# A linear-attention and dense-block kernel: w_in loaded 512 columns at a time, unit one's own term as products, and another written order

## The chip, the cores and the metric

The kernel runs on one core of a Trainium2 chip. A core has TensorE (PE, with its weight loads shown apart as PEld), VectorE (DVE), ScalarE (ACT), GpSimd (POOL) and SyncE (SP), each with an instruction queue of its own, and 16 DMA engines. The metric is the device time of one execution in microseconds (us), as the median of several runs.

## What is computed

Two blocks follow each other. The first is a linear attention with decay, over 4 batches, 8 heads, 768 steps and a head size of 48; the second is a dense block on its 3072 x 384 output:

```python
for t in range(S):
    kt, vt, rt = (k[:, :, t], v[:, :, t], r[:, :, t])
    cur = np.einsum('bhd,bhe->bhde', u[None] * kt, vt)
    y[:, :, t] = np.einsum('bhd,bhde->bhe', rt, state + cur)
    state = w[None, :, :, None] * state + np.einsum('bhd,bhe->bhde', kt, vt)
...
h = x @ w_in            # 384 -> 2048
g = h - np.tanh(h)
return (g @ w_out).astype(np.float32)
```

r, k, v, w and u are float32; w_in and w_out come as float64 (6.3 MB each) and are turned into float32 on the chip. The term with u, `cur`, is called the own term here: it adds to each step's output what the step's own k and v give.

## The kernel before, in words

**Units.** A unit is 64 steps of two batches with all heads; there are 24. Its chain: r, k and v are loaded (`fetch`, L644, two transfers each, one for each batch; for units zero and one one of them is ACT's, otherwise both are SP's); TensorE transposes r and k (`turn`, L656); DVE scales r with the powers of w into rT (L660) and ACT or DVE makes kT (L692, L665); TensorE multiplies rT with the state (`from_state`) and rT with kT (`levels`); DVE copies the products under the causal mask into `at` (L830); TensorE multiplies `at` with v (`outputs`) and k with v (`to_state`), all of these through `put`, L606; ACT copies the outputs into `xt` and `rest` (L765), and DVE or ACT updates the state (L792, L795). From unit twelve on r and k come already spread over DVE's transposes.

**The own term** has two forms. Units with a number under `OWN` (L35) use products: ACT multiplies kT by w times u (`own_k`, L709, four instructions), TensorE makes 16 more products (`own_levels`), and DVE copies their diagonal into `at` (L821). The others multiply r, k and u on DVE (L696, L824), sum over the head (L700), and ACT writes the diagonal (`diagonal`, L704, eight instructions).

**Tiles.** A tile is a block of two units' outputs (256 rows) by 256 columns of w_in. TensorE makes h in two halves of three products each (L217); ACT makes an arctan, two tanh, a square and a relu (L229 to L235); DVE makes g (L242 to L246); TensorE multiplies g with w_out (L254, or L307 in a form with seven products for eight, whose sums POOL prepares). The first six blocks are gone through in three passes over 4, 4 and 8 of the sixteen groups of 128 columns, the other six one by one.

**Weights.** w_in and w_out come in 16 pieces (`Weights`): for each n, n % 4 of 0 and 1 are 256 columns of w_in each, 2 and 3 are 256 rows of w_out. A piece of w_in comes in four transfers, alternately issued by SP (48 partitions, 288 KB) and POOL (16 partitions, 96 KB), in rows of 256 x 8 bytes, into one of four staging buffers `st`. `convert` turns it into float32: DVE twice (L185, L186), ACT twice (L187, L188), DVE three times (L189 to L191).

**What sets the order.** `lay_out` makes a list of tasks, each an engine's step with the tasks it comes after. The string `ORDER` (L45) then names them one by one, two characters each, and `Plan.written` emits them in that order; so each engine's queue is that order, restricted to the engine. An instruction waits for what it reads and for what it overwrites. Numbers beyond the tasks stand for the fillings: products of the identity with itself (`fills`, L534, 512 or 256 columns) that nobody reads, and one for reading the flag that chooses a general path. Transfers of SP and ACT take turns at eight counters; each waits until the transfer eight before it, of either, has landed.

## Time and profile before

| | us |
|---|---|
| runs shown: median, lowest, highest (3) | 582.31, 581.24, 583.12 |
| the profiled execution | 582.57 |
| its span, first to last instruction | 580.8 |
| busy: PE, DVE, ACT, POOL | 562.5, 429.9, 404.3, 199.9 |
| HBM read, written | 31.66 MB, 4.72 MB |
| mean granted TensorE clock | 0.998 |

The profiled execution gives the page and the trace; times in them count from the span's start. A row of a timeline has the start, the time taken, engine, line, operation and tiles, and in brackets the idle time ahead of it with what ended it. `x4` counts instructions; each product of float32 operands shows as two, and some records can be missing. In the chain of work, "issue" is time in which an engine waited for nothing that the profile shows. A busy engine may be one whose instructions are long; TensorE's ends are modelled.

### The profile page before, as it was taken

The numbers are of one execution on the slowest core, as the hardware profiler recorded it, in microseconds if no ns is written. First come the engines' busy times: TensorE is split into PE (matmuls) and PEld (weight loads), VectorE is DVE, ScalarE is ACT, GpSimd is POOL, SyncE is SP. The second block draws the span as 40 slices with busy tenths as digits, with TensorE's granted clock in tenths as the row PEclk, the third lists the DMA queues.
The fourth block names the chain that finished last, engine by engine and source line by source line (L and its number), as shares of the span: only waits on it lengthen the run. The fifth ranks groups of instructions, "written<-read, shape, count | busy, mean of one in ns | idle before, by whom it ended". The sixth has DMA issues, their size and how long they took to land.

```text
span 580.8 us, 14137 instructions
## 1 busy us (share of the span) xinstructions
PE 562.5 (97%) x5487; PEld 480.4 (83%) x5487; DVE 429.9 (74%) x720; ACT 404.3 (70%) x926; POOL 199.9 (34%) x366
## 2 busy tenths in 40 slices
PE   7699999999999999999999999999999999999995
PEld 4467777777776789999888889989999988999994
DVE  4899878999998787967699796567676766454534
ACT  2699999999977566545884787577577568765550
POOL 5201111300000233546256184273455253463430
PEclk9999999999999999999999999999999999999999
DMA  8987857594620000132344451441233000010001
GB/s 137 171 199 145 140 117 118 120 173 109 142 64 5 1 1 1 28 56 44 54 67 85 61 105 23 68 89 17 45 63 61 2 21 16 5 30 2 19 11 32
DMA packets 138549, 38.48 MB, mean 66 GB/s; under 512 B 130761, under 2 KB 132905, under 8 KB 138473
## 3 DMA queue, kind: packets, MB, share of 16 engines
q1 hardware_dynamic: 130140, 29.71, 28.7%
q0 software_dynamic: 4992, 6.99, 5.3%
q10 hardware_dynamic: 3340, 0.79, 0.9%
q8 instruction: 45, 0.74, 0.5%
q14 instruction: 32, 0.25, 0.2%
HBM read 31.66 MB, written 4.72 MB: 63 GB/s over the span
## 4 chain that ended last, share of the span: by engine, by line
PE 87%; DMA 4%; ACT 3%; DVE 2%; issue 1%; SPq 1%; POOL 0%; ACTq 0%; DVEq 0%; POOLq 0%
PE h L217 41%; PE p L307 26%; PE o L254 10%; PE yk_ps L606 6%; DMA rt<-in_r_dram 2%; PE x_ps L656 1%; DMA vt<-in_v_dram 1%; DMA xt<-rest 1%; ACT at L704 1%; PE x_ps L606 1%; SPq L644 1%; ACT xt L765 0%; PE p L254 0%; PE x_ps L534 0%; POOL xt L786 0%
## 5 line engine op out<-in xcount | busy, mean ns | idle before, releaser
L217 PE MATMUL h<-xt,w_in_sb 128*128 128x256 f32 x1152 | 267.3, 381 | 0.2 <-DMA xt<-rest 0.2
L217 PEld LDWEIGHTS h<-xt,w_in_sb 128*128 128x128 f32 x1152 | 214.9, 190 | 32.5 <-DVE g L242 1.5
L290 POOL TENSOR_TENSOR sg<-g 128x256 f32<-128x256 f32 x69 | 55.1, 800 | 197.7 <-DVE g L246 130.1
L242 DVE TENSOR_TENSOR g<-h,th 128x512 f32<-128x512 f32 x96 | 65.8, 686 | 67.9 <-ACT tg L233 25.2
L229 ACT ACTIVATE s<-h 128x512 f32<-128x512 f32 x96 | 57.1, 594 | 54.3 <-PE h L217 47.2
L307 PE MATMUL p<-mixed,sg 128*128 128x192 f32 x426 | 92.3, 327 | 0.0
L244 DVE TENSOR_TENSOR tg<-s,tg 128x512 f32<-128x512 f32 x96 | 69.3, 724 | 29.2 <-ACT s L224 19.4
L233 ACT ACTIVATE tg<-h 128x512 f32<-128x512 f32 x96 | 56.9, 594 | 41.9 <-PE h L217 29.9
L246 DVE COPY_PREDICATED g<-small,tg 128x512 f32<-128x512 int32 x96 | 72.0, 761 | 12.0 <-ACT small L235 9.0
L231 ACT ACTIVATE th<-h 128x512 f32<-128x512 f32 x96 | 56.7, 593 | 32.7 <-PE h L217 32.6
L307 PEld LDWEIGHTS p<-mixed,sg 128*128 128x128 f32 x426 | 73.3, 190 | 1.3 <-issue 0.3
L307 PE MATMUL p<-w_out_sb,g 128*128 128x192 f32 x284 | 70.4, 330 | 0.3 <-DVE o L335 0.3
L235 ACT ACTIVATE small<-s,smallb 128x512 f32<-128x512 f32 x96 | 68.5, 721 | 1.2
L254 PE MATMUL o<-w_out_sb,g 128*128 128x384 f32 x192 | 67.3, 489 | 0.0
L786 POOL DMA_DIRECT2D xt<-rest x66 | 32.5, 496 | 91.7 <-ACT rest L765 91.1
L224 ACT ACTIVATE s<-s 128x512 f32<-128x512 f32 x96 | 60.7, 633 | 1.4
L307 PEld LDWEIGHTS p<-w_out_sb,g 128*128 128x128 f32 x284 | 50.6, 190 | 3.1 <-DVE o L335 0.6
L254 PEld LDWEIGHTS o<-w_out_sb,g 128*128 128x128 f32 x192 | 35.8, 190 | 19.4 <-DVE parts L267 0.2
L704 ACT ACTIVATE at<-same,du 128x64 f32<-128x64 f32 x184 | 48.2, 342 | 0.5 <-DVE du L700 0.4
L292 POOL TENSOR_TENSOR sg<-sg,g 128x128 f32<-128x128 f32 x69 | 39.1, 569 | 3.1
L294 POOL TENSOR_TENSOR sg<-sg,g 128x128 f32<-128x128 f32 x69 | 37.2, 542 | 3.4
L307 PE MATMUL p<-mixed,g 128*128 128x192 f32 x142 | 34.7, 326 | 0.0
(127 smaller groups left out, 654.1 us busy)
## 6 DMA issues: line engine op xcount, KB each, us to landing
st<-in_moe_w_out_dram SPq DMA_DIRECT2D x8, 768.0 KB, 5.5
st<-in_moe_w_in_dram SPq DMA_DIRECT2D x16, 288.0 KB, 5.9
rt<-in_r_dram SPq DMA_DIRECT2D x46, 96.0 KB, 3.6
vt<-in_v_dram SPq DMA_DIRECT2D x46, 96.0 KB, 3.7
kt<-in_k_dram SPq DMA_DIRECT2D x44, 96.0 KB, 3.2
out_dram<-o POOLq DMA_DIRECT2D x44, 96.0 KB, 2.2
st<-in_moe_w_in_dram POOLq DMA_DIRECT2D x16, 96.0 KB, 5.9
parts<-in_k_dram SPq DMA_DIRECT2D x48, 32.0 KB, 2.1
```

Of the source, the lines that this page charges most:

```text
L217: self.nc.tensor.matmul(t.h2[:, z], self.w_in_sb[:, t.f // 2, kk, z * 128 : (z + 1) * 128], self.xts[t.j][:, kk].rearrange("p b t -> p (b ...
L224: A.activation(t.s, t.s, AF.Square, scale=G3)
L229: A.activation(out, t.h, AF.Arctan, scale=G2)
L231: A.activation(out, t.h, AF.Tanh)
L233: A.activation(out, t.h, AF.Tanh, scale=G1)
L235: A.activation(out, t.s, AF.Relu, bias=self.smallb, scale=-1.0)
L242: V.tensor_tensor(t.g, t.h, t.th, ALU.subtract)
L244: V.tensor_tensor(t.tg, t.s, t.tg, ALU.mult)
L246: V.copy_predicated(t.g, t.small.bitcast(I32), t.tg)
L254: self.nc.tensor.matmul(self.outs[i], t.g2[:, z, i * C : (i + 1) * C], self.w_out_sb[:, t.f + z, :], start=t.first and z == 0, stop=t.last ...
L290: add(t.s4[:, :2], g[:, 0::3], g[:, 1:2].to_broadcast([128, 2, C]), ALU.add)
L307: self.nc.tensor.matmul(ps[bank][:, half * n : (half + 1) * n], a, b, start=t.first and half == 0, stop=t.last, skip_group_check=True)
```

## The change

Three edits. First, `OWN` is 2, so unit one's own term takes the form with products too. Second, where w_in is float64, the two pieces of 256 columns next to each other share one set of four transfers with rows of 512 x 8 bytes, into one staging buffer `si` of twice the size; w_out has two buffers `so`. The four transfers of the first pair are all SP's; in later pairs the smaller two stay POOL's. A pair's transfers come after the conversion of both pieces of the pair before. A piece is then converted from its half of the buffer, in the same steps. Third, `ORDER` is another string throughout; it has 11 fillings (four of 512 columns, six of 256, and the flag's reading) where there were 16 (nine, six and the flag's reading).

```diff
-OWN = 1
+OWN = 2
...
-    "00010J2f2g2h2i2j2k2l2m2n0HbWbX02030K040605bWbWbW2o2q3534363231332r2t0I2s07370A0FbWbX080B0C2u2x2y38392v092w3U0D3C"
+    "00012P2Q2R0K2W2T2S2UbEbF02030I042V2X06bF2Y2o2n2p050A0H0C2a2r2q2s072c082b0B2d2e0J2h092f2u2i2Z2w2g0D3A0EbF2y3D2j3C"
...
-        return self.w_in_sb[:, of], parts
+        return parts
+
+    def wide(self, n):
+
+        return n % 4 < 2 and self.sources[0].dtype == I64
 
     def load(self, n, i, queue):
 
-        dst, parts = self.piece(n)
-        if self.sources[n % 4 > 1].dtype == I64:
+        if self.wide(n):
             if n not in self.staged:
-                self.staged[n] = self.stage.tile([128, self.COLS], I64, name="st", tag="st", bufs=4)
-            dst = self.staged[n].rearrange("p (k f) -> p k f", k=dst.shape[1])
+                self.staged[n] = self.staged[n + 1] = self.stage.tile([128, 2 * self.COLS], I64, name="si", tag="si", bufs=1)
+            dst = self.staged[n].rearrange("p (k f) -> p k f", k=self.d.NK)
+            parts = self.spread(self.sources[0][:, n // 4 * 512 : (n // 4 + 1) * 512])
+        else:
+            dst, parts = self.piece(n)
+            if self.sources[n % 4 > 1].dtype == I64:
+                if n not in self.staged:
+                    self.staged[n] = self.stage.tile([128, self.COLS], I64, name="so", tag="so", bufs=2)
...
+        if self.wide(n):
+            st = st[:, :, n % 2 * 256 : (n % 2 + 1) * 256]
...
-            queues, data = (("SP",), (3.0,)) if n % 4 > 1 else (("SP", "POOL") * 2, (1.2, .95) * 2)
-            of = [add(e, .55, lambda n=n, i=i, e=e: weights.load(n, i, e_of[e]), [converted[n - 4] if n >= 4 else None],
-                      data=x, gated=True) for i, (e, x) in enumerate(zip(queues, data))]
+            wide, freed = weights.wide(n), [converted[n - 4]] if n >= 4 else []
+            queues, data = (("SP",), (3.0,)) if n % 4 > 1 else (("SP", "SP" if n < 2 else "POOL") * 2, (1.3, .98) * 2 if wide else (1.2, .95) * 2)
+            if not wide or n % 4 == 0:
+                of = [add(e, .55, lambda n=n, i=i, e=e: weights.load(n, i, e_of[e]), freed + ([converted[n - 3]] if wide and freed else []),
+                          data=x, gated=True) for i, (e, x) in enumerate(zip(queues, data))]
```

`spread` is the old lines that cut w_in's columns into four parts, as a function. All lines behind them have numbers higher by 13 to 15 in the changed kernel (L606 is L621, L217 is L230, L534 is L547).

SP's queue at its start, before. `rt_106`, `rt_107`, `rt_108` are r of units zero, one and two, `first_k_122` and `_123` k of zero and one, `vt_116` and `_117` v of the same, `kt` k of later units, `ub` u, `st` w_in's staging buffer.

```order
L547 DMA rows<-in_w_dram 4x2x48
L171 DMA st<-in_moe_w_in_dram 48x3x256
L644 DMA rt_106<-in_r_dram 64x8x48
L644 DMA first_k_122<-in_k_dram 64x8x48
L644 DMA vt_116<-in_v_dram 64x8x48
L171 DMA st<-in_moe_w_in_dram 48x3x256
L644 DMA first_k_123<-in_k_dram 64x8x48
L644 DMA rt_107<-in_r_dram 64x8x48
L644 DMA vt_117<-in_v_dram 64x8x48
L568 DMA ub<-in_u_dram 128x384
L644 DMA kt<-in_k_dram 64x8x48 x2
L171 DMA st<-in_moe_w_in_dram 48x3x256
```

The same queue after, behind the first two of the list (`rows` and unit zero's r):

```order
L183 DMA si<-in_moe_w_in_dram 16x3x512
L659 DMA first_k_122<-in_k_dram 64x8x48
L183 DMA si<-in_moe_w_in_dram 16x3x512
L659 DMA vt_116<-in_v_dram 64x8x48
L659 DMA rt_107<-in_r_dram 64x8x48
L183 DMA si<-in_moe_w_in_dram 48x3x512
L659 DMA first_k_123<-in_k_dram 64x8x48
L183 DMA si<-in_moe_w_in_dram 48x3x512
L659 DMA rt_108<-in_r_dram 64x8x48
L659 DMA kt<-in_k_dram 64x8x48 x2
L581 DMA ub<-in_u_dram 128x384
L659 DMA vt_117<-in_v_dram 64x8x48
```

The first pair of w_in pieces now goes out whole ahead of unit one's v; in the row behind these the second half of unit two's r follows.

TensorE from unit zero's outputs to the first dense product, before. `x_ps_150` is the bank of unit one, `x_ps_146` that of units zero and two, `at_133` the masked products of unit one, `h<-ident` a filling.

```order
L606 MATMUL yk_ps<-vt_116,kw_112 64x48 x16
L534 MATMUL h<-ident 128x512
L534 MATMUL h<-ident 128x256
L606 MATMUL x_ps_150<-rT,kT 64x64 x16
L534 MATMUL h<-ident 128x256
L656 MATMUL x_ps_146<-ident,kw_112 128x128 x4
L656 MATMUL x_ps_146<-ident,rt_108 128x128 x4
L606 MATMUL yk_ps<-at_133,vt_117 64x64 x12
L606 MATMUL yk_ps<-at_133,extra_131 64x64 x12
L606 MATMUL yk_ps<-vt_117,kw_113 64x48 x16
L217 MATMUL h<-xt,w_in_sb 128x256 x3
```

And after:

```order
L621 MATMUL yk_ps<-vt_116,kw_112 64x48 x16
L621 MATMUL x_ps_150<-rT,kT 64x64 x16
L547 MATMUL h<-ident 128x512 x2
L671 MATMUL x_ps_146<-ident,kw_112 128x128 x4
L621 MATMUL x_ps_150<-rT,kU 64x64 x16
L671 MATMUL x_ps_146<-ident,rt_108 128x128 x4
L621 MATMUL yk_ps<-at_133,vt_117 64x64 x12
L621 MATMUL yk_ps<-at_133,extra_131 64x64 x12
L621 MATMUL yk_ps<-vt_117,kw_113 64x48 x16
L230 MATMUL h<-xt,w_in_sb 128x256 x3
```

Unit one's own products have come in, and the fillings stand behind its levels; unit two's r is still turned ahead of unit one's outputs.

DVE between unit one's scaling of r and its own copy, after (before, the two conversion steps of one piece stood here, and unit one's rk steps). `si` is w_in's buffer with both pieces.

```order
L675 TENSOR_TENSOR rT<-x_ps_150,power 128x512
L198 TENSOR_SCALAR power<-si 128x768
L199 TENSOR_SCALAR w_in_sb<-si 128x768
L198 TENSOR_SCALAR power<-si 128x768
L199 TENSOR_SCALAR w_in_sb<-si 128x768
L822 TENSOR_TENSOR kw_112<-kt,w_down 128x8x48
L845 COPY_PREDICATED at_133<-before,x_ps_150 128x512
L202 SCALAR_TENSOR_TENSOR w_in_sb<-w_in_sb,si 128x768
L836 COPY_PREDICATED at_133<-same,x_ps_150 128x512
```

The first steps of both pieces now stand ahead of the masked copies of unit one.

More of the change, by code (lines that the diff above doesn't have):

```diff
@@ L177, in convert @@
         V, A = self.nc.vector, self.nc.scalar
[L178 to L183 removed]
+        dst, st = self.piece(n)[0], self.staged.pop(n).rearrange("p (k f) -> p k f", k=self.piece(n)[0].shape[1])
+        if self.wide(n):
+            st = st[:, :, n % 2 * 256 : (n % 2 + 1) * 256]
+        words = st.bitcast(U32).rearrange("p k (f t) -> p k f t", t=2)
+        lo, hi = words[..., 0], words[..., 1]
+        lo_f = st.bitcast(F32).rearrange("p k (f t) -> p k f t", t=2)[..., 0]
+        power = self.stage.tile([128, self.COLS], U32, name="power", tag="power", bufs=2).rearrange("p (k f) -> p k f", k=dst.shape[1])
         bits = dst.bitcast(U32)
```

97 lines of the change are left out of this document (46 added, 51 removed).

## The prediction

> **What bounds the kernel now.** I read the page first: engine totals, the line of clock shares, the chain that ended last.
>
> ```profile
> span 580.8 us, 14137 instructions
> PE 562.5 (97%) x5487; PEld 480.4 (83%) x5487; DVE 429.9 (74%) x720; ACT 404.3 (70%) x926; POOL 199.9 (34%) x366
> PEclk9999999999999999999999999999999999999999
> PE 87%; DMA 4%; ACT 3%; DVE 2%; issue 1%; SPq 1%; POOL 0%; ACTq 0%; DVEq 0%; POOLq 0%
> ```
>
> TensorE is busy for 97% of the span, and 87% of the chain is its own. So a change can save only where TensorE does no useful work. A table by stretches shows where that is, and the same table for line 534 alone shows the products with the identity that only fill a wait.
>
> ```profile
> 25.40:55.70 30.30, 27.26 (x540) 20.52 (x536) 27.80 (x50) 29.44 (x86) 3.43 (x7) 1.00 0.91 182
> 55.70:100.00 44.30, 42.89 (x846) 33.17 (x846) 36.39 (x65) 42.29 (x126) 8.63 (x18) 1.00 0.66 118
> 100.00:150.00 50.00, 50.00 (x315) 36.80 (x314) 46.97 (x74) 47.16 (x98) 6.94 (x14) 1.00 0.65 139
> 150.00:580.80 430.80, 423.47 (x3492) 378.07 (x3490) 302.66 (x503) 275.60 (x594) 170.12 (x287) 1.00 0.22 39
> sum 50.00, PE 13.51 PEld 5.63; mean PE 1.35 PEld 0.56
> ```
>
> Columns: the stretch and its length, busy time of PE, PEld, DVE, ACT and POOL (instructions in brackets), granted clock, DMA share, GB/s; the last row is line 534 in the first 50 us. From 55.7 us TensorE lacks 1.4 us up to 100, nothing up to 150, and 7.3 us after that, most of it the end of the program. The loss sits ahead of 55.7: 13.5 us of filling, and idle time. From 25.4 to 55.7 DVE (27.8 of 30.3 us) and ACT (29.4) are as full as TensorE, and TensorE's 27.3 hold fillings. The chain in order of time says what holds the start:
>
> ```profile
> 4.19 6.26 DMA vt<-in_v_dram
> 15.20 7.33 DMA rt<-in_r_dram
> 22.66 0.63 PE x_ps L656 x4
> 23.29 0.90 PE yk_ps L606 x48
> 24.22 0.50 ACT xt L765
> 24.76 0.68 PE yk_ps L606 x32
> 25.44 1.49 PE h L217 x6
> 27.56 2.21 issue
> 29.77 0.69 PE x_ps L606 x32
> ```
>
> Unit two's r lands at 22.53; its transposes stand on TensorE ahead of unit one's outputs (23.29), from which ACT makes xt (24.22), and the first dense product starts at 25.44. At 27.56 TensorE stands for 2.21 us for nothing that the profile shows.
>
> **The change, part by part.** *Fewer fillings.* They fall from nine of 512 columns and six of 256 to four and six. TensorE's rows:
>
> ```profile
> 16.99 1.56 PE L534 MATMUL h<-ident 128*128 128x512 f32 x4
> 19.02 0.69 PE L606 MATMUL x_ps<-rT,kT 48*64 48x64 f32 x32 [0.47 <-DVE kT L665]
> 33.89 2.74 PE L534 MATMUL x_ps<-ident 128*128 128x512 f32 x6
> 42.45 0.59 PE L534 MATMUL x_ps<-ident 128*128 128x256 f32 x2
> 43.56 0.69 PE L606 MATMUL yk_ps<-rT,state 48*64 48x64 f32 x32 [0.52 <-DVE state L792]
> ```
>
> Three of 512 take 2.74 us, so five fewer are 5 x 0.91 = 4.6 us. But the filling of 16.99 ends at 18.55 and the next product still waits 0.47 us for DVE; the one of 42.45 likewise, 0.52. They cover waits that exist without them, so I cost their removal at nothing by itself: it is a gain only where the waits shorten. 4.6 us is the upper bound if they all do.
>
> *Unit one's own term.* What goes and what comes is shown by rows of units zero and one:
>
> ```profile
> 12.63 0.97 PE L606 MATMUL x_ps<-rT,kU 48*64 48x64 f32 x32 [1.01 <-ACT kU L709]
> 13.66 0.75 DVE L821 COPY_PREDICATED at<-same,x_ps 128x512 f32<-128x512 int32 x1 [1.19 <-PE x_ps L606]
> 15.23 0.55 DVE L696 TENSOR_TENSOR rk<-rt,first_k 128x384 f32<-128x384 f32 x1
> 17.23 0.55 DVE L824 TENSOR_TENSOR rk<-rk,ub 128x384 f32<-128x384 f32 x1
> 17.82 0.55 DVE L700 TENSOR_REDUCE du<-rk 128x8 f32<-128x384 f32 x1
> 18.41 2.02 ACT L704 ACTIVATE at<-same,du 128x64 f32<-128x64 f32 x8 [0.38 <-DVE du L700]
> 11.92 0.40 ACT L709 ACTIVATE kU<-kT,w_u 128x128 f32<-128x128 f32 x1 [1.58 <-POOL w_u L564]
> 12.23 0.97 ACT L709 ACTIVATE kU<-kT,w_u 128x128 f32<-128x128 f32 x3
> ```
>
> DVE loses 3 x 0.55 and gains 0.75: -0.9. ACT loses 2.02 and gains 0.40 + 0.97: -0.7. TensorE gains 16 products, 0.69 to 0.97 us, in a stretch where it fills: nothing on the path.
>
> *w_in.* Four transfers fetch what eight did; rows of 4 KB replace 2 KB; the first four are all SP's, where POOL issued half. Bytes stay. DVE's conversions are the same four large steps a piece. SP's queue changes: the w_in transfers now stand ahead of unit one's k, of u and of unit one's v, and unit two's r is split, its second half behind them all. At most eight transfers of SP and ACT are under way; in the program that second half waits until ACT's half of unit one's v has landed.
>
> ```profile
> 12.00 0.60 ACTq L644 DMA_DIRECT2D vt<-in_v_dram  x1
> 17.52 0.39 POOL L739 COPY extra<-vt 128x96 f32<-128x96 f32 x1 [4.39 <-DMA vt<-in_v_dram]
> DMA to landing us min/median/max: 2.7/4.4/7.4
> DMA to landing us min/median/max: 3.4/5.9/7.7
> ```
>
> The last two rows are r's and w_in's transfers. ACT's half of v is issued at 12.00, behind the same ACT steps in both, and has landed by 17.52. So unit two's r goes out at about 17.5 and, at the median 4.4, lands at 21.9 where it landed at 22.53: -0.6 us. Bounds: 2.7 gives 20.2, but then unit one's own copy on DVE decides. I put the last w_in issue at 10 us (SP's issues are 0.6 us each, with the landings they wait for); at the median 5.9 it lands at 16. Between that and the own copy DVE has four conversion steps (0.55), unit two's kw (0.55), the masked copy (0.75), a step of 0.95 and the copy itself: about 4.9 us with overlaps, so 21 us at best, -1.5. The maximum 7.4 gives 24.9, +2.4. I take -0.6, the median's.
>
> [...]
>
> *The order behind the first product.* I compare the same place in both: unit five's masked copy on DVE and the outputs behind it (TensorE, 55.68). Both orders have done seven half tiles of h and two of o by then.
>
> ```profile
> 24.00 0.69 DVE L660 TENSOR_TENSOR rT<-x_ps,power 128x512 f32<-128x512 f32 x1 [1.36 <-ACT kT L692]
> 54.04 0.74 DVE L830 COPY_PREDICATED at<-before,x_ps 128x512 f32<-128x512 int32 x1
> 24.00:54.80 30.80, 28.26 (x51) 1.00 0.92 183
> ```
>
> DVE has 28.3 us of work in 30.8. The changed order has four instructions fewer there: three of unit two's rk steps are already done ahead of it, two short conversion steps and one masked copy are elsewhere, two long conversion steps and a kw come in: -3 x 0.5 - 2 x 0.5 - 0.6 + 2 x 0.9 + 0.5 = -0.8 us; with the flag's step, -0.9. The idle 2.5 us depend on loads, on ACT and on the 2.21 us stall; the new order holds shorter fillings there (one of 512 and three of 256 where there were three and two, about 1.2 us less). I take half, -1.3; bounds 0 and -2.5, and +1 if a load is late under the denser first transfers.
>
> *Behind 55.7* TensorE is full in both, so what is won ahead is kept. Bounds: 1 us either way for the waits in the 1.4 and 7.3 us above.
>
> **Sum.** The profiled execution took 582.57, 1.77 more than its span of 580.8. -0.6 - 0.9 - 1.3 = -2.8, so 579.8 against it. The median of the runs shown, 582.31, is 0.3 lower: 579.5.
>
> **The rivals.** *No change.* The same bytes must land before unit two's r as before, so the first term may be zero; and ACT is nearly full up to 150 us (42.3 of 44.3, 47.2 of 50), and the new order leaves it some tile steps (about three of 0.6 us) for later, so the idle time won may come back as waits for ACT. Only -0.9 is left: 581.4. Against it: TensorE is at 50.00 of 50 beside that ACT.
>
> *Slower by w_in.* DVE takes up w_in at one place, ahead of unit two's kw and unit one's masked copy. If the last transfer lands at 20.5 and not 16, unit one's outputs follow at 26.1 (4.9 us of DVE, 0.7 of products), 2.8 us behind the 23.29 of now; the point from which it is slower by more than the noise is about 21. At 22 it is 4.3 late less 0.9: 585.7. For it: twice the bytes in one transfer. Against: the longest landing among w_in's rows, 7.7, gives 18.
>
> *Slower by the clock.* The new order has few fillings between 5 and 16 us. Two rows of the end show what rest does to the clock:
>
> ```profile
> 572.00 2.74 PE L254 MATMUL p<-w_out_sb,g 128*128 128x384 f32 x8
> 570.00:581.00 11.00, 4.74 (x22) 3.33 (x20) 3.25 (x8) 0.32 (x1) 0.00 (x0) 0.86 0.16 42
> ```
>
> The last product ends at 574.74 and the mean clock of 0.86 over 11 us, as full and half speed, puts the fall at about 578: 3.2 us of rest. If a rest of that length comes ahead of the first dense product, some 9 us of TensorE's own small products run at half speed, somewhat over half of them on the path: 579.5 + 5 = 584.5. Its point is a rest over 3.2 us; the longest I find without the fillings is about 2.3, between the first filling and unit zero's r. [...]
>
> **How the numbers follow.** A measurement of this kernel tells about 0.3%, 1.75 us, from no change: faster is below 580.56, slower above 584.06. Forecast 579.5: 0.58. More than that, all idle time gone (577 or less): 0.09. No change: 0.20. Slower by w_in 0.07, by the clock 0.06. Faster 0.67, same 0.20, slower 0.13. The range takes in -1.5 - 0.9 - 2.5 - 1 at the low end, 576.4, and at the high end the no-change case with a late load (+2.4 - 0.9): 583.8.
>
> **What would show it.** Right: unit two's r transposes at about 22, the first dense product at 24.5 to 25, unit five's masked copy at about 51, no PE idle time behind 56 that was not there. Wrong: a DVE wait for w_in behind 18 us; a granted clock under 1.00 between 5 and 40 us; ACT named for TensorE's waits between 56 and 150 us; the first product or unit five's copy no earlier than 25.4 and 54.0.

## The result, and the profile after

The changed kernel takes 599.21 us (median of 4 runs, 598.32 to 603.08), the kernel before 581.77 in the same comparison: 1.030 times as long (95% interval 1.027 to 1.033). The forecast of 579.5 has the wrong sign. The profiled execution is the one of 598.32. Its page, and the table by stretches (columns as in the prediction):

```profile
span 596.5 us, 14188 instructions
PE 567.8 (95%) x5509; PEld 485.1 (81%) x5509; DVE 436.6 (73%) x718; ACT 403.2 (68%) x922; POOL 199.2 (33%) x356
```

```profile
0.00:25.40 25.40, 17.05 (x208) 11.62 (x209) 10.42 (x23) 6.17 (x14) 6.55 (x32) 1.00 0.99 128
120.00:134.00 14.00, 7.05 (x23) 5.25 (x22) 8.24 (x12) 4.77 (x8) 2.16 (x5) 0.76 1.06 193
```

The last stretch in the kernel before:

```profile
120.00:134.00 14.00, 14.00 (x57) 10.50 (x56) 13.02 (x20) 13.05 (x30) 0.00 (x0) 1.00 0.69 141
```

It held 14.00 us of products. Now it holds 7.05, at a granted clock of 0.76, while the DMA engines are full (share 1.06). Counted by TensorE's products still to come, fillings left out, the changed kernel is 7 us behind at its first dense product (32.42 us for 25.37), about 8 between 50 and 110 us, 18 at 130 us, and wins about 2 back by the end; the span is 15.7 us longer. (The counts in between are estimates, since the two orders do not do the same work at the same place.) So there are two losses: one ahead of the first dense product, where the prediction looked for a gain, and one near 122 us, where it saw next to nothing to win or lose.

**The first loss, ahead of the first dense product.** TensorE's rows:

```profile
8.25 1.12 PE L671 MATMUL x_ps<-ident,rt 128*128 128x128 f32 x4 [2.45 <-DMA rt<-in_r_dram]
11.17 1.09 PE L671 MATMUL x_ps<-ident,first_k 128*128 128x128 f32 x4 [1.80 <-DMA first_k<-in_k_dram]
19.39 1.08 PE L671 MATMUL x_ps<-ident,first_k 128*128 128x128 f32 x4 [1.45 <-DMA first_k<-in_k_dram]
24.48 3.77 PE L547 MATMUL h<-ident 128*128 128x512 f32 x4
32.42 1.53 PE L230 MATMUL h<-xt,w_in_sb 128*128 128x256 f32 x6
```

Three waits for loads in a row, and products at half speed: two fillings take 3.77 us where three took 2.74 before. The clock records of this trace begin to show the full clock at 28.1 us; the shares of 1.00 above it mean only that no record stands there. Unit one's k, turned at 19.39, was turned 5.6 us earlier in the kernel before:

```profile
13.83 0.65 PE L656 MATMUL x_ps<-ident,first_k 128*128 128x128 f32 x4
```

VectorE in the changed kernel, and SP's queue:

```profile
23.60 0.95 DVE L198 TENSOR_SCALAR power<-si 128x768 uint32<-128x768 uint32 x1 [1.33 <-DMA si<-in_moe_w_in_dram]
24.47 0.94 DVE L199 TENSOR_SCALAR w_in_sb<-si 128x768 uint32<-128x768 uint32 x1
25.33 0.94 DVE L198 TENSOR_SCALAR power<-si 128x768 uint32<-128x768 uint32 x1
26.19 0.94 DVE L199 TENSOR_SCALAR w_in_sb<-si 128x768 uint32<-128x768 uint32 x1
27.05 0.55 DVE L822 TENSOR_TENSOR kw<-kt,w_down 128x384 f32<-128x384 f32 x1
27.51 0.75 DVE L845 COPY_PREDICATED at<-before,x_ps 128x512 f32<-128x512 int32 x1
29.38 0.73 DVE L836 COPY_PREDICATED at<-same,x_ps 128x512 f32<-128x512 int32 x1 [0.29 <-PE x_ps L621]
```

```profile
12.37 0.62 SPq L183 DMA_DIRECT2D si<-in_moe_w_in_dram  x1
24.50 0.60 SPq L659 DMA_DIRECT2D rt<-in_r_dram  x1
```

VectorE's queue stands at w_in until 23.60. It is ready for w_in only 1.33 us earlier, since it had to wait for unit one's k too. So two late loads stand one behind the other, and the wait for w_in itself is the smaller part. The two first steps of a piece, 0.55 us before, take 0.94, and those of both halves stand ahead of unit two's kw and unit one's masked copy. The last w_in transfer goes out at 12.37; unit two's r goes out at 24.50, behind ACT's half of unit one's v, which was issued at 13.23 and landed only at 24.48. Unit two's r holds nobody here: TensorE turns it at 29.24 without a wait.

**The second loss, at 122 us.** TensorE, then GpSimd and SP, and the tile `rest` (the six small transfers that fill a block's xt) between 112 and 134 us:

```profile
130.32 4.60 PE L230 MATMUL h<-xt,w_in_sb 128*128 128x256 f32 x12 [6.95 <-DMA xt<-rest]
```

```profile
117.86 3.26 POOL L801 DMA_DIRECT2D xt<-rest  x6 [12.18 <-ACT rest L780]
121.11 1.05 POOL L183 DMA_DIRECT2D si<-in_moe_w_in_dram  x2
```

```profile
118.25 0.34 SPq L183 DMA_DIRECT2D si<-in_moe_w_in_dram  x1
119.33 0.61 SPq L183 DMA_DIRECT2D si<-in_moe_w_in_dram  x1
```

```profile
DMA to landing us min/median/max: 6.8/9.6/9.9
```

Between the six, SP puts out the two larger transfers of w_in's third pair; GpSimd's two go out behind the six. The six take 9.6 us where they took 1.6 before, TensorE rests 6.95 us, and the clock is at half speed for the next products (0.50 from 127.09 to 133.92 us; 4.60 us for twelve, 2.75 in the kernel before). The third pair comes just here because of the one buffer. VectorE's last step that reads the pair before it ends at 118.18, and SP's first transfer goes out at 118.25:

```profile
117.23 0.95 DVE L203 SCALAR_TENSOR_TENSOR power<-si,power 128x768 uint32<-128x768 uint32 x1
```

In the kernel before, the same six went out at 108.67, and the product on that tile came at 123.09:

```profile
108.67 2.86 POOL L786 DMA_DIRECT2D xt<-rest  x6 [13.90 <-ACT rest L765]
123.09 2.75 PE L217 MATMUL h<-xt,w_in_sb 128*128 128x256 f32 x12
```

```profile
DMA to landing us min/median/max: 1.6/1.6/1.6
```

There one of the eight transfers of w_in's third pair went out at 104.00 and had landed by 107.99; the other seven went out from 113.42 on, behind the six.

### The profile page after: what moved, and what is told of

Its sections match the earlier page's. It is cut to its first block, busy times and chain, and to the rows that moved or that the text cites. A ratio compares the mean times of both kernels' runs of the same rounds, so it can differ in the third digit from the quotient of the medians.

```text
span 596.5 us, 14188 instructions
## 1 busy us (share of the span) xinstructions
PE 567.8 (95%) x5509; PEld 485.1 (81%) x5509; DVE 436.6 (73%) x718; ACT 403.2 (68%) x922; POOL 199.2 (33%) x356
## 3 DMA queue, kind: packets, MB, share of 16 engines
q1 hardware_dynamic: 128988, 30.11, 29.3%
## 4 chain that ended last, share of the span: by engine, by line
PE 71%; DVE 4%; issue 1%; ACT 0%; DVEq 0%
PE h L230 35%; PE p L320 28%; PE yk_ps L621 4%; PE o L267 4%; DVE power L198 1%; DVE w_in_sb L199 0%; DVE w_out_sb L204 0%; PE p L267 0%; DVE g L255 0%; DVE tg L257 0%; DVE parts L280 0%; DVE power L203 0%; ACT th L244 0%; DVE g L259 0%; DVE w_out_sb L202 0%
## 5 line engine op out<-in xcount | busy, mean ns | idle before, releaser
L230 PE MATMUL h<-xt,w_in_sb 128*128 128x256 f32 x1152 | 268.0, 383 | 9.5 <-DMA xt<-rest 8.1
L230 PEld LDWEIGHTS h<-xt,w_in_sb 128*128 128x128 f32 x1152 | 216.7, 191 | 41.8 <-issue 8.9
L303 POOL TENSOR_TENSOR sg<-g 128x256 f32<-128x256 f32 x69 | 55.7, 809 | 203.2 <-DVE g L259 165.1
L257 DVE TENSOR_TENSOR tg<-s,tg 128x512 f32<-128x512 f32 x96 | 70.9, 740 | 20.4 <-ACT s L237 18.8
L719 ACT ACTIVATE at<-same,du 128x64 f32<-128x64 f32 x176 | 45.7, 341 | 0.2
L305 POOL TENSOR_TENSOR sg<-sg,g 128x128 f32<-128x128 f32 x69 | 40.4, 588 | 4.0
L307 POOL TENSOR_TENSOR sg<-sg,g 128x128 f32<-128x128 f32 x69 | 38.7, 562 | 4.1
L320 PE MATMUL p<-w_out_sb,sg 128*128 128x192 f32 x142 | 34.8, 327 | 0.0
```

The source lines that it names most:

```text
L230: self.nc.tensor.matmul(t.h2[:, z], self.w_in_sb[:, t.f // 2, kk, z * 128 : (z + 1) * 128], self.xts[t.j][:, kk].rearrange("p b t -> p (b ...
L257: V.tensor_tensor(t.tg, t.s, t.tg, ALU.mult)
L303: add(t.s4[:, :2], g[:, 0::3], g[:, 1:2].to_broadcast([128, 2, C]), ALU.add)
L320: self.nc.tensor.matmul(ps[bank][:, half * n : (half + 1) * n], a, b, start=t.first and half == 0, stop=t.last, skip_group_check=True)
```

## The experiments

Each kernel stands beside runs of the kernel before on the same chip; "before" below is their median. Theory one was the clock, theory two the data that the first conversion waits for.

**Fillings put back into the changed kernel.**

```diff
-[256] r of unit zero | k of unit zero | ... | [256] k of unit one
+[512 x3, 256] r of unit zero | [512 x2] k of unit zero | ... | [512 x4] k of unit one
```

> The changed kernel with seven more filling products at the start (three 512-column ones ahead of unit zero's r, two ahead of its k, four in the place of one 256-column one ahead of unit one's k); nothing else differs. Theory one, the clock: the first dense product comes at 32.4 us and not at 25.4 because TensorE, with holes of 2.45, 1.80 and 1.45 us at its start, is granted the full clock only at 28.1 us, and every product until then takes twice as long. Then the full clock is granted by 8 us, the first dense product comes at 26 to 27.5 us and the time falls by 5 to 6 us, to 593 to 594. Theory two, the data: w_in's pair is whole only at 23.5 us, VectorE's and ScalarE's seven steps behind it take some 6.5 us, and no clock changes that. Then the full clock is granted, but the first dense product stays at 30 us or later and the time at 597 to 598. The loss at 122 to 134 us should stay in both.

603.24 us (before 582.12), 1.038 (1.030 to 1.045): slower still. TensorE:

```profile
4.58 3.27 PE L547 MATMUL h<-ident 128*128 128x512 f32 x8
19.58 0.63 PE L671 MATMUL x_ps<-ident,first_k 128*128 128x128 f32 x4 [1.03 <-DMA first_k<-in_k_dram]
27.40 0.48 PE L621 MATMUL x_ps<-rT,kT 48*64 48x64 f32 x3 [4.59 <-issue]
35.95 1.53 PE L230 MATMUL h<-xt,w_in_sb 128*128 128x256 f32 x6
```

The full clock came by 5 us (eight product instructions of fillings take 3.27 us, where two of half their width took 1.22), and unit one's k was no earlier: 19.58 for 19.39. A stall of 4.59 us for nothing that the profile shows came in; without it the first dense product would stand at 31.4, by which theory one explains about 1 us of the first loss. This is an estimate and not a clean test, since the clock was lost again behind the stall (two fillings from 27.81 us on took 3.78 us). But up to the stall the clock was full (eight product instructions of fillings took 3.70 us at 14.85), and unit one's k came no earlier for it. Neither theory expected the stall; it comes back below.

**Fillings taken out of the kernel before.**

```diff
-[512, 256] | [512 x3] | [512, 256] | [512, 256] | [256] first dense product
+[512, 256] | [256]    | [256]      | [512 x2]   |       first dense product
```

> The kernel before with its ten filling products ahead of the first dense one cut to the six that the changed kernel has (one 512 and one 256, then 256, 256 and two of 512); nothing else differs. Theory one, the clock: the half clock stays until 20 us or later, the first dense product moves from 25.4 to 29 to 31 us and the time from 582 to 586 to 588. Theory two, the data: fillings stand in waits that are there anyway, w_in comes as before, the first dense product stays within 1 us of 25.4 and the time within 1 us of 582.

582.31 us (before 582.12), 0.999 (0.996 to 1.001).

```profile
6.92 1.11 PE L656 MATMUL x_ps<-ident,rt 128*128 128x128 f32 x4 [1.11 <-DMA rt<-in_r_dram]
25.62 1.56 PE L217 MATMUL h<-xt,w_in_sb 128*128 128x256 f32 x6
```

The clock did fall (a 128-column group at 1.11 us, and 0.60 before, in the transposes of unit zero's r), and the first dense product moved by 0.25 us. The fillings cost nothing and, in that order, save nothing.

**The third pair written twenty tasks later**; in SP's queue:

```diff
 vt_118<-in_v_dram
-si<-in_moe_w_in_dram 48x3x512
 vt_118<-in_v_dram
+si<-in_moe_w_in_dram 48x3x512
 si<-in_moe_w_in_dram 48x3x512
```

> The changed kernel with the four transfers of w_in's third pair of pieces written some twenty tasks later, behind unit fourteen's v and the dense product that waits at 130 us; nothing else differs. Theory three: the wait of 6.95 us at 130.3 us and the half clock that follows it (127 to 134 us) are there because the six small transfers of the xt tile stand among 1.2 MB of w_in and land 9 us after their issue where 2 to 2.5 us are usual. Then the six land in under 3 us, the wait goes, the clock stays full there and the time falls by 8 to 9 us, to 590 to 591. Rival: the wait only moves, since the conversion of that pair then comes late and the dense products on it wait, or VectorE's queue stands at it; then the time stays above 596.

600.23 us (before 582.12), 1.031 (1.027 to 1.036): no change. The transfers went out beside the six as ever, and the wait of 6.96 us for xt stayed. It tests nothing: with a wait as long as the changed kernel's 6.95 us, the later place in SP's queue held nothing back.

**The small parts of the first pair back in GpSimd's queue.**

```diff
-("SP", "SP" if n < 2 else "POOL") * 2
+("SP", "POOL") * 2
```

> The changed kernel with the two small parts of w_in's first pair put out by GpSimd's queue, as the later pairs are; nothing else differs. Theory: that SyncE's queue puts out the whole first pair alone holds the loads written behind it (unit zero's and unit one's k land at 11.0 and 19 us, before at 8.3 and 13.5), so w_in and k land 1 to 2 us earlier and the time falls by 1 to 2 us. Rival: the bytes in flight and the clock decide, not the queue that issues them; k lands within 0.5 us of where it was and the time stays within 1 us of 599.

598.54 us (before 582.12), 1.028 (1.024 to 1.032): as the changed kernel. That SyncE issues the first pair alone costs nothing that these runs can tell. (In the kernel before, unit one's k had landed at 12.29 us, not at 13.5.)

**w_in's first pair in two pieces again**, the second piece and its conversion later, the small parts in GpSimd's queue.

```diff
-return n % 4 < 2 and self.sources[0].dtype == I64
+return n > 1 and n % 4 < 2 and self.sources[0].dtype == I64
...
+    both = self.stage.tile([128, 2 * self.COLS], I64, name="si", tag="si", bufs=1)
+    self.staged[0], self.staged[1] = both[:, : self.COLS], both[:, self.COLS :]
```

> The changed kernel with w_in's first pair loaded again in two pieces of 256 columns, each in its own half of the staging buffer, the first piece at the places of the wide transfers, the second one and its conversion at the places that they have in the kernel before; the other pairs stay wide. Theory two, the data: the wide pair puts 1.57 MB of w_in ahead of unit one's k, v and the first conversion (0.79 MB before), so w_in lands at 23.5 us and the chain behind it (two first steps of both halves at 0.94 us each, then the rest) ends 8.9 us later. Then unit one's k lands by 16 us, the first conversion starts at 16 to 18 us with steps of 0.55 us, the first dense product comes at 26 to 28 us and the time falls by 4.5 to 6 us, to 593 to 595, with the half clock as long as now. Theory one, the clock: the first dense product stays past 31 us and the time within 1.5 us of 599.

595.91 us (before 583.19), 1.023 (1.017 to 1.028): by the ratios 0.7%, 4 us, less than the changed kernel; 4.5 to 6 were expected. Two rows of TensorE, then a first conversion step, which reads a contiguous half, and unit one's own copy on VectorE:

```profile
20.60 3.74 PE L550 MATMUL h<-ident 128*128 128x512 f32 x4
28.52 1.53 PE L233 MATMUL h<-xt,w_in_sb 128*128 128x256 f32 x6
```

```profile
18.31 0.55 DVE L201 TENSOR_SCALAR power<-si 128x768 uint32<-128x768 uint32 x1
25.47 0.73 DVE L839 COPY_PREDICATED at<-same,x_ps 128x512 f32<-128x512 int32 x1 [3.05 <-PE x_ps L624]
```

The two intervals overlap a little (1.027 to 1.033 for the changed kernel), but the trace agrees: 3.9 us of the 7.0 are won, the steps take 0.55 us again, and VectorE no longer waits for w_in. What holds the rest is partly the changed order itself: two fillings of 512 columns, at half speed, stand on TensorE ahead of unit one's own products, and VectorE waits 3.05 us for these. In the changed kernel that wait is 0.29 us, since w_in is later still. So the half clock and the place of the fillings cost something once w_in comes early; how much was not measured.

**The third pair behind the xt tile**, all four transfers by GpSimd.

```diff
+("POOL", "POOL") * 2 if n == 8 else ("SP", "SP" if n < 2 else "POOL") * 2
```

> The changed kernel with all four transfers of w_in's third pair of pieces (1.57 MB) put out by GpSimd's queue, behind the six small transfers of the xt tile; the earlier try moved them only within SyncE's list, where nothing held them back, and they went out at the same time. Theory three: the six small transfers take 9 us because SyncE puts w_in out between them. Then they land within 4 us of their issue, the wait of 7 us at 130 us falls under 1 us, the clock stays full and the time falls by 8 to 9 us, to 590 to 591. Rival: the wait moves to w_in, which then lands later than its conversion can wait, or the six are late for another reason; the time stays above 596.

593.08 us (before 583.19), 1.017 (1.012 to 1.022): by the ratios 1.3%, 7.5 us, less. The six land in 1.6 us, as expected, and the wait for xt at 122 us is gone; the time is 2 us over what was expected. But VectorE and TensorE:

```profile
133.48 1.81 DVE L198 TENSOR_SCALAR power<-si 128x768 uint32<-128x768 uint32 x2 [2.92 <-DMA si<-in_moe_w_in_dram]
```

```profile
137.67 4.31 PE L230 MATMUL h<-xt,w_in_sb 128*128 128x256 f32 x12 [4.17 <-DVE g L255]
```

The rival came in half: w_in now lands too late, VectorE's queue stands at it, and TensorE waits 4.17 us for a step queued behind the four slow ones. With one buffer for a pair, its load starts only when both conversions of the pair before have read it (the rows at 118 us above); in this order that is just when xt is due, and one of the two is late.

**Both edits.**

> Both edits in one kernel: w_in's first pair in two pieces and the third pair behind the xt tile on GpSimd's queue. If the two losses are separate their gains add: 584 to 587, with 1 to 3 us of the half clock at the start left over against the kernel before. If one only covers the other (what is late next comes late anyway), 589 or more.

591.02 us (before 583.19), 1.012 (1.007 to 1.018): 1.7% less, where the two edits alone give 0.7 and 1.3. The gains add nearly, so the two losses are separate in the main. The time is still over the 584 to 587 of that reading, since each edit gave less than was expected of it; the wait behind w_in (4.51 us now) stays.

**The bytes alone, in the kernel before**; in SP's queue, and likewise in GpSimd's:

```diff
 st<-in_moe_w_in_dram 48x3x256
+st<-in_moe_w_in_dram 48x3x256
 rt_106, first_k_122, vt_116
 st<-in_moe_w_in_dram 48x3x256
+st<-in_moe_w_in_dram 48x3x256
 first_k_123, rt_107, vt_117, ub, kt x2
...
-st<-in_moe_w_in_dram 48x3x256 x2
```

> The kernel before with the four transfers of w_in's second piece put out each right behind its match of the first piece; buffers, steps, fillings and the rest of the order are as they were. The bytes ahead of the first conversion double as in the changed kernel, but no step of VectorE changes its form or place. Theory two: the first conversion's data and unit one's k come 3 to 5 us later, the first dense product at 28 to 30 us, the time is 585 to 587. Theory one (the clock alone), or that the order of the transfers is covered: the first dense product within 1 us of 25.4, the time within 1 us of 582.

589.98 us (before 583.19), 1.011 (1.005 to 1.017).

```profile
19.41 1.11 PE L656 MATMUL x_ps<-ident,first_k 128*128 128x128 f32 x4
31.78 1.56 PE L217 MATMUL h<-xt,w_in_sb 128*128 128x256 f32 x6
```

Nothing but the place of four transfers changed, and the first dense product moved from 25.37 to 31.78, almost the changed kernel's 32.42. Doubling w_in's bytes ahead of the first conversion is enough for a loss of that size; it cost 3 us more than was expected. The path is another one, though. ACT's queue shows it:

```profile
18.02 0.60 ACTq L644 DMA_DIRECT2D vt<-in_v_dram  x1
18.66 0.48 ACT L562 COPY w_down<-h 128x384 f32<-128x384 f32 x1 [1.45 <-DMA st<-in_moe_w_in_dram]
```

ACT issues unit one's v only at 18.02 (at 12.00 in the kernel before), its next step has stood for 1.45 us, by the profile for a w_in transfer, and TensorE waits 1.68 us for that step at 19.28, a wait that the changed kernel does not have. The products were slow as well: a 128-column group took 1.11 us at 19.41, and 0.60 at 28.66. So the run shows what the bytes can cost, and not that they act by the changed kernel's path.

**w_in narrow in all pairs**: the kernel before with `OWN = 2` and the changed order.

```diff
-si x4 (pieces 8 and 9)
+st x4 (piece 8), ahead of the six of xt; st x4 (piece 9), behind them
```

> The changed kernel with the w_in part of the change taken back in all four pairs: pieces of 256 columns in the four staging buffers of the kernel before, the small parts by GpSimd's queue; the first piece of the third pair is put out ahead of the xt tile's six small transfers, the second behind them. Unit one's own term as products and the written order stay as changed. Theory two (the wide pairs cost the time, by their bytes ahead of everything at the start and by their one buffer at 118 us): both losses go, what is left is the half clock until some 24 us (about 2 us); 583 to 586. Rival: the new written order and the fewer fillings themselves cost what is left in the kernel with both edits (591.0 against 582); then 589 or more.

592.36 us (before 582.19), 1.015 (1.011 to 1.018): this is the rival. TensorE still waits 2.33 us for unit one's k, until 17.50, and 5.57 us for xt.

**The same with the fillings of before.**

> The kernel of the run before with fillings as in the kernel before: three of 512 ahead of unit zero's r in the place of one of 256, one of 512 and one of 256 behind its k. Full clock by 8 us; if the half clock at the start still costs 2 us in that kernel, the first dense product comes 1.5 to 2.5 us earlier and the time is 581 to 584. If the half clock lies beside waits for data, the time stays within 1 us of that kernel's.

596.32 us (before 582.19), 1.022 (1.018 to 1.026): 4 us worse, not better. The clock is full early (a 128-column group takes 0.60 us at 8.34), but unit one's k is no earlier (TensorE turns it at 18.10 behind a wait of 4.36 us), and behind that wait the clock is half again (1.09 us for such a group). So a full clock at the very start does not help there.

**Unit one's products alone, in the kernel before.**

```diff
-OWN = 1
+OWN = 2
```

> The kernel before with unit one's own term as TensorE products (sixteen more, one masked copy in the place of two multiplications, a reduction and sixteen scalings) and nothing else: the steps take the places of those that they replace. The prediction put this at 0 to 0.9 us gained: 581 to 582.5 beside 582. If the half products or the masked copy stand in unit one's chain, 582.5 to 584.

583.16 us (before 582.19), 1.0024 (1.0003 to 1.0045): no gain; 0.2 to 2.6 us lost.

**Narrow, the third pair written behind the xt tile.**

> The kernel with the w_in part taken back in all pairs, with both pieces of the third pair now written behind the six small transfers of the xt tile (in the run before the first piece stood ahead of them, and TensorE still waited 5.5 us for xt at 123 us). If the xt transfers are late only because w_in is put out with them, the wait falls under 1.5 us and the time from 592.4 to 586 to 588. Rival: w_in's third pair then comes late for VectorE, as when it was wide, and the time stays at 590 or more.

590.77 us (before 581.26), 1.016 (1.012 to 1.020): no better. SP's transfers still went out beside the six, two of them among these, and the six took 7.6 us; the same slip as with the twenty tasks.

**Narrow, and the third pair kept behind the xt tile by GpSimd's queue.**

```diff
-(("SP", "POOL") * 2, ...)
+(("POOL" if n in (8, 9) else "SP", "POOL") * 2, ...)
```

> The kernel with w_in narrow in all pairs, and now all eight transfers of the third pair in GpSimd's queue behind the six of the xt tile (in the run with them written behind, SyncE still put two of them out between the six, and these took 7 us). If the bytes of w_in beside the xt tile make the wait of 5 us at 120 us, the six land within 2 us of their issue, the wait falls under 1 us, and the time from 590.8 to 583.5 to 586. Rival: the third pair then comes late for VectorE, whose queue stands at it as it did with the wide pair; 589 or more.

586.17 us (before 583.38), 1.0041 (1.0017 to 1.0065). TensorE, and the six transfers:

```profile
121.14 2.75 PE L217 MATMUL h<-xt,w_in_sb 128*128 128x256 f32 x12
134.93 2.86 PE L217 MATMUL h<-xt,w_in_sb 128*128 128x256 f32 x12 [1.78 <-DVE g L242]
```

```profile
DMA to landing us min/median/max: 1.6/1.6/1.7
```

The wait is gone, and w_in, in pieces and in four buffers, still comes nearly in time (one wait of 1.78 us). From 1.016 to 1.004 by the queue of four transfers alone: this is what the second loss costs with narrow w_in.

**The head of one order with the rest of the other** (w_in narrow in both, joined at the first dense product). The first kernel has the head of the kernel before and the rest of the narrow one with its third pair written behind the xt tile (1.016); the second has the changed head.

> The same kernel, but all tasks up to the first dense product in the order of the kernel before (its transfers, fillings and steps; unit one's own term as products), and from there on in the changed order. Theory four: with narrow w_in the start's loss is the written order of the transfers, which puts unit one's and two's r and w_in's later parts ahead of unit one's k; then the first dense product comes at 25 to 27 us and the time is 5 to 6 us under that of the run beside it, at 581 to 583. Theory five: the order behind the first dense product costs most; the time is within 2 us of the run beside it.

592.58 us (before 581.26), 1.019 (1.017 to 1.022).

> The reverse: all tasks up to the first dense product in the changed order (w_in narrow, six fillings), and from there on in the order of the kernel before. Theory four: the start alone costs 5 to 7 us, and nothing behind it gives them back: 587 to 590. Theory five: the time is within 2 us of the kernel before, 581 to 584.

583.58 us (before 581.26), 1.0034 (1.0017 to 1.0051). Theory five holds and theory four falls: the old head gains nothing on the 1.016. With narrow w_in the changed order costs little ahead of the first dense product (it comes at 28.90 in the second kernel, but only 2 us are lost at the end, and 1.0024 is the price of unit one's products alone), and much behind it. Where, the first kernel's rows on TensorE and on VectorE show:

```profile
24.35 1.56 PE L217 MATMUL h<-xt,w_in_sb 128*128 128x256 f32 x6
31.43 0.83 PE L606 MATMUL yk_ps<-at,vt 64*64 64x64 f32 x32 [2.10 <-DVE at L830]
51.03 4.19 PE L217 MATMUL h<-xt,w_in_sb 128*128 128x256 f32 x12 [2.33 <-DMA xt<-rest]
```

```profile
29.25 1.03 DVE L185 TENSOR_SCALAR power<-st 128x768 uint32<-128x768 uint32 x2 [3.93 <-DMA st<-in_moe_w_out_dram]
30.66 0.72 DVE L830 COPY_PREDICATED at<-before,x_ps 128x512 f32<-128x512 int32 x1
```

The first dense product comes at 24.35, a microsecond earlier than before. Then VectorE's queue stands 3.93 us at w_out's first piece, the masked copy behind it is late, and TensorE loses 2.10; then xt is late at 51 us. At 124.10 TensorE has waited 3.93 us more; the profile names a w_in transfer. At all three places the order counts on data earlier than it lands.

**The second half's first steps behind the first half's last**, in the changed kernel; on VectorE:

```diff
-power<-si, w_in_sb<-si (second half)
 kw, masked copy, the rest of the first half
+power<-si, w_in_sb<-si (second half)
```

> The changed kernel itself (wide w_in), with the two first conversion steps of the second half and ScalarE's two behind them moved behind the last step of the first half; nothing else differs. If the first dense product is set by VectorE's chain behind w_in's landing at 23.5 us, as the trace reads (32.4 - 23.5 = 8.9 us, of it 1.9 us for these two steps), it comes 1.5 to 2 us earlier, at 30.5 to 31, and the time falls by 1 to 2 us, to 597.5 to 598.5. If the clock or unit one's k sets it, it stays within 0.5 us of 32.4 and the time within 1 us of 599.

600.97 us (before 583.38), 1.030 (1.025 to 1.034). The first dense product came 0.74 us earlier, at 31.68, not 1.5 to 2; then TensorE waited 2.38 us for ScalarE, on which the moved steps stood ahead of the state's. On VectorE the masked copy did come 1.5 us earlier (25.97), but its own copy then waited 1.08 us for products that stand behind TensorE's fillings. What the chain alone costs stays open.

**The slow steps walked the other way**, 256 columns outside and three row groups inside.

```diff
-V.tensor_scalar(power, hi, ...)
+V.tensor_scalar(power.rearrange("p k f -> p f k"), hi.rearrange("p k f -> p f k"), ...)
```

> The changed kernel, with the two first conversion steps (VectorE, from uint32 words of the staging buffer) walking the same 768 numbers with the 256 columns outside and the three row groups inside, in the source and in the destination; nothing else differs. In the changed kernel these steps take 0.94 us from si and 0.55 us from so, both of 128 x 768 numbers. Theory: the slow form is that of the operands' walk (a source of 3 x 256 to a destination of one run of 768), and an even outer count on both sides brings back 0.55 us; then four steps ahead of the first dense product give 1.6 us of the chain behind w_in's landing, the first dense product comes at 30.5 to 31.5 and the time falls by 0.5 to 1.5 us. Rival: the buffer's stride alone makes it slow; the steps stay at 0.94 us or longer and the time at 599 or more.

603.94 us (before 582.02), 1.039 (1.034 to 1.045).

```profile
24.02 0.95 DVE L201 TENSOR_SCALAR power<-si 128x768 uint32<-128x768 uint32 x1 [1.35 <-DMA si<-in_moe_w_in_dram]
24.79 0.88 DVE L202 TENSOR_SCALAR w_in_sb<-si 128x768 uint32<-128x768 uint32 x1
25.48 0.93 DVE L201 TENSOR_SCALAR power<-si 128x768 uint32<-128x768 uint32 x1
26.18 0.95 DVE L202 TENSOR_SCALAR w_in_sb<-si 128x768 uint32<-128x768 uint32 x1
```

By their own length the steps stay near 0.94 us, as the rival has it; from start to start they take 0.70 us, between the 0.86 of the changed kernel and the 0.46 of the contiguous steps above. The same edit made w_out's steps, whose buffer has no gaps, slower (0.90 us, not 0.55). So the walk matters, and this one is no remedy: no run shows that an even outer count on both sides brings back 0.55 us. That the gap alone makes the steps slow is neither shown nor excluded.

**The changed order from 270 us on only**, behind the order of the kernel before, with unit one's products.

> The kernel before with unit one's products, in its own order up to block four's first product of the last pass (near 270 us) and in the changed order from there on. Counted by the dense work still to come, the changed kernel gains 1.7 us on the one before between 240 us and the end. If that gain is the order's, this kernel is 1 to 2 us faster than the one with unit one's products alone (583.2), at 581 to 582; if it is only how the two orders line up, 583 or more.

581.96 us (before 583.38), 0.9975 (0.9953 to 0.9997). It is the only kernel here that is faster than the one before, by 0.2 to 2.7 us, so it is barely clear of the noise, and it is one of eighteen that were tried.

## Why the prediction was wrong

*Fewer fillings* "at nothing by itself": right for the start. The kernel before with six in the place of ten takes 0.999 of its time. Where the changed order puts them is another matter, which the kernel with the first pair in pieces shows (3.05 us on VectorE).

*Unit one's own term*, -0.9 on VectorE: the sum counted it as a gain, and there is none; alone it costs 0.03 to 0.45%.

*w_in, the landing.* This step failed first. "I put the last w_in issue at 10 us; at the median 5.9 it lands at 16": it was issued at 12.37 and VectorE got it at 23.6. The bytes stay, over the program; ahead of the first conversion they double, from 0.79 to 1.57 MB. Medians of a trace in which 0.79 MB stood there were used for one in which 1.57 did. The next term hung on it: "ACT's half of v has landed by 17.52, so unit two's r goes out at about 17.5". The link was right, to the hundredth (landed 24.48, out at 24.50), and the time was 7 us off. But the sum took unit two's r for the path to the first dense product, and it was not: TensorE turned it without a wait, behind VectorE's steps. The bound of +2.4 came from the longest landing of the same trace and was no bound. The working also names w_in's transfers as standing ahead of unit one's k and gives that no term; k was turned 5.6 us later (19.39 for 13.83). That doubled early bytes alone can cost as much, the kernel before with them shows, by another path.

*"DVE's conversions are the same four large steps a piece"*: wrong in their form. The working did count the four first steps of both pieces ahead of unit one's own copy, at 0.55 us each, and put 4.9 us from w_in's arrival to the end of that copy; it was 6.5 (23.60 to 30.11). The slower steps make 1.6 us of it, four times 0.86 for 0.46 from start to start. In the program the source in `si` is three rows of 256 with gaps between them, and the destination three rows without gaps; from `so` neither side has gaps. The trace has 0.94 us for the first and 0.55 for the second. Walked with 256 outside on both sides, the steps from `si` took 0.70 from start to start, still not the 0.46 of the contiguous ones, and those from `so` rose to 0.90. What in the form decides was not shown.

*The order behind the first product*, -1.3 with an upper bound of +1: wrong. I counted instructions on VectorE and took it that a wait shortens where the order is tighter. The two joined kernels show the reverse: in the changed order the steps stand closer to the landing of their data, and VectorE's queue, 3.93 us at w_out's first piece, held the masked copy written behind it, which cost TensorE 2.10.

*"Behind 55.7 nothing", within 1 us*: wrong, by some 9 us at one place. That TensorE was full there was true because block five's xt was filled 14 us ahead of its product (108.67, 123.09), with seven of the eight transfers of w_in's third pair behind it. The changed order leaves some 5.5 us (117.86, 123.4), and the one buffer lets the third pair go out just then. I had looked only at how full the engines were, not at how long before its use each transfer was issued.

*The rivals.* That of w_in had the mechanism of the first loss: it gives unit one's outputs 5.6 us behind w_in, 29.2 us with w_in at 23.6; they came at 30.20. It had nothing of the second loss. It got 7 in 100, on the strength of a landing time taken from the emptier queue. That of the clock had its condition wrong: no rest of 3.2 us occurred at the start, and with rests of 2.45, 1.80 and 1.45 us the half clock stayed until 28 us. It decided little there, as far as the runs tell, but followed the rest of 6.95 us that began at 123.4 and cost 1.9 us on the next twelve products. "No change" was not near.

**How the loss divides.** By ratios, with the places chosen here: 1.030 changed; 1.015 with w_in narrow; 1.004 with its third pair also behind the xt tile. So about half lies in the wide pairs and a good third in the third pair beside the xt tile. What the last 0.4% is made of (products of unit one, the start's order, w_out's first piece) was not taken apart. The losses do not simply add: wide w_in and the changed order each delay the first conversion, and with one cured the other still holds.

## What to carry to other kernels

When a load is made larger, count the bytes that stand ahead of the first thing that waits, and not the bytes of the program: here they went from 0.79 to 1.57 MB, and w_in, put at 16 us from the old trace, reached VectorE at 23.6. For every transfer that a new order moves, compare the time from issue to first use with the landing time under the load beside it; here 14 us of slack for transfers of 1.6 us kept TensorE full, and 5.5 us for transfers of 9.6 did not. Putting the third pair twenty tasks later in SP's queue left the wait as it was (6.96 us); putting it behind the six in GpSimd's queue brought the six back to 1.6 us.

## What the runs showed of the hardware

The six small transfers of block five's xt tile take 1.6 us where w_in's transfers stand behind them (the kernel before, whose DMA share from 108 to 113 us is 0.07, and the wide and the narrow kernel with the third pair in GpSimd's queue). They take 6.8 to 9.9 us in the changed kernel, and 6.9 to 7.9 in the narrow one with the third pair written behind them, where SP puts out w_in among them.

In the changed kernel's trace the clock falls to half 3.7 us after TensorE's last product ahead of the wait for xt (123.37 us, 127.09) and stands there for 6.83 us; at the end of the kernel before it falls 3.3 us after the last product (574.74, 578.07). The changed kernel's 4.28 us of unbroken products at its start, from 1.52 to 5.80, were not followed by full speed in the profiled execution: the groups of 128 columns took 1.06 to 1.12 us up to 20.5, and 0.64 at 28.05. In the kernel with the third pair twenty tasks later, whose products begin alike, such a group took 0.66 us at 8.10, and behind a wait of 2.79 us 1.09 at 11.54.

TensorE's long stalls (over 1.2 us) with "issue" as their only reason are 2.21 us in the kernel before, 2.22 with fewer fillings, 4.59 with the fillings put back and 2.49 in the changed kernel. In the two traces of the kernel before and the changed one the records of products, weight loads and TensorE's semaphore and like instructions ahead of the stall number 705 and 1217, 512 apart, and the page has DMA queues for instructions:

```profile
q8 instruction: 45, 0.74, 0.5%
```

As an estimate: if this queue is TensorE's, which the page does not say, its 45 packets of 16 KB for some 11 thousand records would be one for every 247. What TensorE waits for in these stalls no run shows.
